# Loading the later queries of an attention–convolution kernel through SyncE in 1 KB f32 runs, and reordering their rows in the exponentials

## The chip, the cores and the metric

The kernel runs on one core of a Trainium2 chip. The time is device time in microseconds (us) from one launch, median of three runs. The profile is one execution of the same program taken by the hardware profiler. Engines are named as the profile names them: PE (TensorE, with PEld for its weight loads), DVE (VectorE), ACT (ScalarE), POOL (GpSimd), SP (SyncE, here only a queue that issues DMAs).

## The reference, cut to what matters

There are 8 batches, 12 heads, 448 rows and 64 elements per head. Attention is a softmax with an extra one in the denominator; its output, 448 x 768 per batch, goes into a gated layer with a circular convolution over the rows.

```
scores = q @ k.T / 8                      # per batch and head, 448 x 448
e      = exp(scores)
x      = (e / (sum(e) + 1)) @ v           # heads side by side: 448 x 768   (max shift cancels)
proj   = x @ w_proj                       # 768 x 2304
x1, x2, x3 = proj split in three
y      = x1 * x3 * irfft(rfft(x2) * rfft(filter))
out    = y @ w_out                        # 448 x 768, f32
```

## The kernel before, in words

**Units.** Heads are taken in pairs, six pairs to a batch, 48 pairs in all; pair i is pair i % 6 of batch i // 6. Per pair the scores stand transposed: keys on the partitions, the 448 queries along the free side. Keys 0 to 383 of each head are three tiles of 128 rows (t = 1, 2, 3, both heads at once); the last 64 keys of the two heads share a fourth tile (t = 0). `scores(t)` (L766 to L773) writes them to PSUM, `exps(t)` (L775 to L784) turns them to bf16 in SBUF with the scale folded in: 128 x 896 for t = 1, 2, 3 and 128 x 448 for t = 0. `out_rests` and `out_rest` (L792 to L810) multiply by v; the exponentials are the stationary operand there, 128 queries at a time, so **the order of the queries in an exponential tile is the order of the rows of x**. A column of ones beside v gives the sums, and `norm` (L812 to L824) divides, on DVE, into the tile `xb`.

**Getting x transposed.** The dense layer wants x with channels on the partitions (`xT`). For batches in `XALL`, and for the first five pairs of batches 2, 3 and 4, this is a DMA transpose issued by SP, three pairs (or two) at a time (`x_dma`, L886 to L893). For all other pairs PE transposes four blocks of 128 x 128 (`x_pe`, L898) and DVE or ACT copies them out of PSUM (`x_back`, L905 and L907): all of batches 0 and 1 and the last pair of batches 2, 3 and 4, so 15 pairs.

**Loading q, k and v.** Batches 0 and 1 (`staged`) come in f32 through SP into a ring of staging rooms, are cast on POOL (the first pair on DVE) and turned on PE. There a partition p of the q room holds the four queries 4p to 4p+3 of a head, one run of 1 KB; the copy out of PSUM (L488 to L493) puts the 448 columns back in row order. Batches 2 to 7 (`loaded`, L524 to L602) take k and v the same way through five rooms, cast on POOL, but are turned by DMA (`k_turn`). Their q is loaded by POOL-issued DMAs that cast on the way (`q_load`, L533): one strip of 112 consecutive rows for all twelve heads, in runs of 64 f32 elements, 256 bytes. A DMA transpose per strip (`q_turn`, L539) puts it in place already in row order. Four strips make a batch; batch 2 loads each in two halves, so there are 28 such loads and 28 such turns.

**Dense layer.** Per batch: folds of xT on DVE (L947 to L955), a projection P (L978), spectra Z (L1005) with products on DVE (L1019, L1025), the gates G (L1051, with L1063 and L1066), the inverse transform I (L1090) with its unfolding, and the output O (L1163, L1175).

**Order.** Nothing is scheduled by hand line by line. Every step is a task with an engine, a cost, a priority (`want`), needs, and buffers taken and given; `Plan.run` (L72) walks a model of the five engines and of two DMA queues and gives each engine the first ready task by priority among the next 160. The result is one fixed, in-order program per engine, with semaphore waits. The constants at the top of the kernel (L270 to L291) only move priorities: `ATT` and `SLOT` for each batch's attention, `DENSE`, `PACE` and `FOLD` for its dense layer, `LEAD` and `AHEAD` for loads. `LOAD` also is an earliest time in the model for the five weight loads and the filter load that POOL issues. `LANDING` and the argument `run` model how long a DMA takes to land and how the two queues share the transfers.

Of the kernel before, what the change touches and what calls it, by code (L numbers as in the profile page):

```python
# [23 lines left out]
NHP = H // 2  # L24
SCALE = 1.0 / float(np.sqrt(DH))
# [16 lines left out]
class Plan:  # L42
# [8 lines left out]

    WINDOW = 160
    LAT = {"PE": 0.2, "ACT": 0.22, "DVE": 0.2, "POOL": 0.15, "SP": 0.0}
    LANDING = 1.8
    OPEN = 8
    BEGIN = 0.75

# [11 lines left out]
    def add(self, eng, cost, want, emit, need=(), make=(), take=(), give=(), dma=0.0, run=256, n=1, after=0.0, begun=(), late=0.0):  # L69
        self.tasks.append((want, len(self.tasks), eng, cost, emit, need, make, take, give, dma, after, run, n, begun, late))  # L70
# [186 lines left out]
def kernel(  # L257
# [13 lines left out]
    MAGIC = 12582912.0  # L271
    NSTAGED = 2
    SPIN = 38
    EARLY1 = 3.56
    ATT = [0.74, 31.12, 90.92, 107.97, 154.61, 193.46, 231.91, 282.14]
    SLOT = [2.70, 6.66, 5.08, 5.83, 4.70, 0.35, 4.90, 4.50]
    DENSE = [45.16, 85.16, 124.09, 170.16, 216.54, 256.31, 315.08, 409.78]
    PACE = [2.27, 2.24, 1.74, 2.16, 1.15, 2.13, 0.54, 0.88]
    FOLD = [-0.15, 0.76, -31.49, -25.60, 10.65, 0.32, 9.43, 0.88]
    BPS = 1.26  # L280
    RE1 = 16.91
    WT = 2.03
    FT = 18.78
    HALVED = (2,)
    AHEAD = [0, 0, 46.94, 46.01, 34, 34, 34, 34]
    LEAD = [-8.41, 6.91, 5.34, 23.10]
    LOADS = ((1, 0), (1, 1), ("F", None), (0, None), (2, None), ("O", None))
    LOAD = [36.34, 20.13, 13.48, 39.00, 39.88, 46.37]
    STEP = 4.27
    XALL = (5, 6, 7)  # L290
    FOLD0 = (39.83, 49.48, 37.97)  # L291

    const = ctx.enter_context(tc.tile_pool(name="const", bufs=1))
    wts = ctx.enter_context(tc.tile_pool(name="wts", bufs=1))
# [25 lines left out]
    kT = [const.tile([128, NHP, 4, 128], BF16, name=f"kT{i}") for i in range(2)]  # L320
    qT = [const.tile([128, NHP, S], BF16, name=f"qT{i}") for i in range(2)]
    vn = [const.tile([128, NHP, 7, DH + 1], BF16, name=f"vn{i}") for i in range(2)]
    ks = const.tile([128, NHP, 128], BF16, name="ks")

    es = [const.tile([128, 2 * S + REM], BF16, name=f"e{i}") for i in range(6)]
    er = [const.tile([128, S + REM], BF16, name=f"er{i}") for i in range(2)]
# [2 lines left out]


    KNAT, ROOM = NHP * 4 * 128, 1280
    nat = const.tile([128, max(KNAT + NST * D, 8 * ROOM)], BF16, name="nat")
    kn = nat[:, 0:KNAT].rearrange("p (g t c) -> p g t c", g=NHP, t=4)
    qn = nat[0:SP, KNAT : KNAT + NST * D].rearrange("p (t c) -> p t c", t=NST)
    nf = nat.bitcast(F32)

    def stage(g, at, n):
        o = g % 4 * ROOM + at
# [15 lines left out]
    def bank(hy):  # L354
        i = plan.banks[hy][0]
        return psum[:, 512 * i : 512 * i + 512]
# [167 lines left out]
    def loaded(b):  # L524

        i0 = b * NHP
        want = tau(i0) - AHEAD[b]
        parts = 2 if b in HALVED else 1
        size = NHP // parts
# [13 lines left out]

        def k_turn(hp):
# [6 lines left out]
        n = 0  # L551
        for part in range(parts):
            gs = slice(size * part, size * part + size)
            for st in range(NST):
                room = [("c" + w, i0 - 2) for w in "kqv"] if b == NSTAGED else [("qturn", b - 1, st)]
                add("POOL", 0.8 if parts > 1 else 0.95, want + STEP * n, lambda st=st, gs=gs: q_load(st, gs), need=room,
                    make=[("qn", b, part, st)], dma=1.3 / parts)
                n += 1
                add("SP", 1.3, want + 6.0 + STEP * n, lambda st=st, gs=gs: q_turn(st, gs), need=[("qn", b, part, st), last],
                    make=[("qturn", b, st)] + [("qT", i0 + i) for i in range(gs.start, gs.stop)], dma=0.6 / parts, late=0.7)  # L560
# [11 lines left out]

        for hp in range(NHP):
            g = i0 + hp
            for n, (name, x) in enumerate((("k", k), ("v", v))):
                slot = 2 * (g - NHP * NSTAGED) + n
                at = (KNAT + NST * D) // 2 + 384 * (slot % 5)
                src = nf[:, at : at + 384]
                old = slot - 5
                room = [("c" + "kv"[old % 2], NHP * NSTAGED + old // 2)] if old >= 0 else [  # L580
                    ("c" + w, i) for w in "kqv" for i in range(NHP * NSTAGED - 2, NHP * NSTAGED)]
# [177 lines left out]
    def attention(i):  # L759
# [15 lines left out]
        def exps(t):  # L775
            if t:
                P["e"][t] = e = es[(3 * i + t - 1) % 6]
                nc.scalar.activation(  # L778
                    e[:, 0 : 2 * S].rearrange("p (u n) -> p u n", u=2), pair(("sc", ("S", i, t)))[:, :, 0:S], AF.Exp,
                    scale=SCALE,  # L780
                )
            else:
                P["e"][t] = e = er[i % 2]
                nc.scalar.activation(e[:, 0:S], bank(("hy", ("S", i, t)))[:, 0:S], AF.Exp, scale=SCALE)  # L784

        def out_banks():
            return pair(("op", i))[:, :, 0 : NST * (DH + 1)].rearrange("p u (n d) -> p u n d", n=NST)
# [442 lines left out]
    with (  # L1230
# [54 lines left out]
            need=[("c" + x, g) for x in "kqv" for g in range(NHP * NSTAGED - NHP, NHP * NSTAGED - 2)], make=["zero kn"])  # L1285
        for (part, ch), at in zip(LOADS, LOAD):
            if part == "F":
                add("POOL", 1.6, at, filter_load, need=["ft", "bps"], make=["filt"], take=[("yT", "F")], dma=4.1, run=2600, n=3, after=at)
            elif part == "O":
                add("POOL", 0.95, at, wout_load, make=["wout"], dma=6.9, run=2600, after=at)  # L1290
            elif ch is None:
                add("POOL", 0.95, at, lambda part=part: wproj_load(part, None), make=[("w", part, 0), ("w", part, 1)], dma=6.9,
                    run=2600, after=at)
            else:
                add("POOL", 0.7, at, lambda part=part, ch=ch: wproj_load(part, ch), make=[("w", part, ch)], dma=3.5, run=2600, after=at)
        more_tables()
        filter_spectrum()
        for i in range(n_batches * NHP):
# [34 lines left out]
```

## Time and profile before

| what | value |
|---|---|
| median of 3 runs | 387.96 us (386.69 to 388.25) |
| span of the profiled execution, first to last instruction | 384.6 us |
| outside the span, median less span | 3.4 us (2.1 to 3.7 over the runs) |
| PE busy | 367.6 us |
| ACT busy, DVE busy, POOL busy | 264.9, 258.4, 113.9 us |
| bytes moved by DMA | 59.12 MB in 136109 packets |
| packets under 512 bytes | 100925 |
| POOL-issued queue / SP-issued queue, packets | 37184 / 98640 |

The page gives a span for the profiled execution and no launch time of its own; the difference to the median is what lies around the span. A line of the groups reads: line of the kernel, engine, operation, output <- inputs, shape, count, busy us, mean ns of one, then the idle time of the engine before them with what ended it. "L898" is line 898 of the kernel shown above. A matmul's duration is longer than the distance to the next one, since matmuls are pipelined; the chain of waits counts only the distance.

### The profile page before, as it was taken

Reading aid. Unit: us, or ns where it says so; the run is one execution under the profiler, and the core shown is the slowest. Engines: PE = TensorE matmul, PEld = TensorE weight load, DVE = VectorE, ACT = ScalarE, POOL = GpSimd, SP = SyncE. Lnnn points to the kernel's source line nnn. Section 1 sums busy time; section 2 is a strip of 40 time slices with the busy share of each in tenths; the row PEclk is TensorE's granted clock in tenths of the full one; section 3 lists DMA queues with packets and bytes.
Section 4 is the critical chain, followed back from the end, with each engine's and each line's share of the span. In section 5 each row is a group of like instructions: output and inputs, shape, how many; then the busy total and the mean of one; then the engine's idle time right before and its main releaser. Section 6 shows DMA issues by size and latency. Waiting matters only on the chain.

```text
span 384.6 us, 9596 instructions
## 1 busy us (share of the span) xinstructions
PE 367.6 (96%) x3720; PEld 235.1 (61%) x3720; DVE 258.4 (67%) x676; ACT 264.9 (69%) x460; POOL 113.9 (30%) x232
## 2 busy tenths in 40 slices
PE   8786999999999999999998999999999999999995
PEld 7554775566765566655754576555665567557652
DVE  6576749955788548974399758584577845971870
ACT  6686769545887869787767768687678875543543
POOL 5783942422762644543364331100000000000000
PEclk9998999999999999999999999999999999999999
DMA  8999999999999999999999952932302033103004
GB/s 209 241 205 250 212 215 214 150 184 194 241 213 196 173 290 233 198 151 258 264 248 127 232 134 77 201 84 82 84 3 43 22 103 84 43 0 124 0 2 164
DMA packets 136109, 59.12 MB, mean 154 GB/s; under 512 B 100925, under 2 KB 132480, under 8 KB 136064
## 3 DMA queue, kind: packets, MB, share of 16 engines
q1 hardware_dynamic: 98640, 48.74, 57.9%
q0 software_dynamic: 37184, 9.54, 27.8%
q8 instruction: 29, 0.48, 0.5%
q10 hardware_dynamic: 240, 0.23, 0.2%
q14 instruction: 16, 0.13, 0.1%
HBM read 43.86 MB, written 11.01 MB: 143 GB/s over the span
## 4 chain that ended last, share of the span: by engine, by line
PE 78%; DVE 12%; DMA 4%; issue 1%; ACT 1%; POOL 1%; SPq 1%; DVEq 0%; POOLq 0%
PE psum L1051 22%; PE psum L978 16%; PE psum L1163 14%; PE psum L804 9%; PE psum L771 7%; DMA filt<-in_moe_filter_fft_dram 3%; PE psum L1005 2%; DVE t L1019 2%; PE psum L773 2%; PE psum L1090 2%; DMA nat<-in_q_dram 2%; DVE yh L1025 2%; DVE g L1066 1%; PE psum L796 1%; DVE cv L1119 1%
## 5 line engine op out<-in xcount | busy, mean ns | idle before, releaser
L778 ACT ACTIVATE e<-psum 128x896 bf16<-128x896 f32 x144 | 125.4, 921 | 21.6 <-PE psum L771 20.7
L1051 PE MATMUL psum<-xT,wproj_bf 128*128 128x448 bf16 x576 | 121.4, 352 | 0.3 <-DVE g L1066 0.3
L1051 PEld LDWEIGHTS <-wproj_bf 128*128 128x128 bf16 x576 | 54.0, 97 | 44.6 <-issue 2.0
L978 PE MATMUL psum<-wproj_bf,xf 128*113 128x384 bf16 x384 | 69.7, 327 | 0.0
L978 PEld LDWEIGHTS <-xf 128*113 128x113 bf16 x384 | 49.4, 132 | 13.7 <-issue 2.2
L1163 PE MATMUL psum<-wout_bf,yT 128*128 128x384 bf16 x288 | 51.9, 326 | 0.1
L1063 ACT CAST x<-psum 128x448 bf16<-128x448 f32 x48 | 25.6, 534 | 33.7 <-PE psum L1051 33.5
L804 PE MATMUL psum<-vn,e 128*128 128x65 bf16 x1152 | 45.3, 195 | 0.0
L600 POOL CAST vn<-nat 128x192 bf16<-128x192 f32 x72 | 28.8, 428 | 47.5 <-DMA nat<-in_v_dram 32.7
L1066 DVE TENSOR_TENSOR g<-x,psum 128x448 bf16<-128x448 bf16 x48 | 29.5, 615 | 19.5 <-PE psum L1051 19.0
L804 PEld LDWEIGHTS <-e 128*128 128x128 bf16 x1152 | 39.6, 98 | 2.8
L771 PE MATMUL psum<-qT,kT 64*128 64x448 bf16 x288 | 41.2, 358 | 0.0
L1175 ACT COPY osb<-psum 128x384 f32<-128x384 f32 x56 | 26.1, 483 | 20.5 <-PE psum L1163 20.1
L1163 PEld LDWEIGHTS <-yT 128*128 128x128 bf16 x288 | 27.4, 98 | 19.1 <-DVE yT L1134 0.8
L1019 DVE TENSOR_TENSOR t<-xs,hrs 113x768 bf16<-113x768 bf16 (+1 forms) x64 | 34.5, 577 | 1.6 <-ACT xs L1013 1.6
L817 DVE TENSOR_SCALAR rec<-psum 128x8 f32<-128x8 f32 x48 | 7.7, 161 | 40.5 <-PE psum L804 35.5
L819 DVE TENSOR_TENSOR xb<-psum,rec 128x512 bf16<-128x512 f32 x48 | 33.2, 691 | 1.7
L990 DVE CAST x<-psum 113x384 bf16<-113x384 f32 x32 | 17.7, 553 | 23.9 <-PE psum L978 23.7
L534 POOL DMA_DIRECT2D nat<-in_q_dram x28 | 24.8, 888 | 28.6 <-DMA wproj_bf<-in_moe_w_proj_dram 11.2
L1013 ACT CAST xs<-psum 113x384 bf16<-113x384 f32 (+1 forms) x64 | 28.0, 491 | 4.3 <-PE psum L1005 4.2
L992 ACT CAST x<-psum 113x384 bf16<-113x384 f32 x32 | 15.3, 480 | 21.8 <-PE psum L978 21.5
L784 ACT ACTIVATE er<-psum 128x448 bf16<-128x448 f32 x48 | 26.7, 556 | 2.9 <-PE psum L773 2.8
(109 smaller groups left out, 440.5 us busy)
## 6 DMA issues: line engine op xcount, KB each, us to landing
nat<-in_k_dram SPq DMA_DIRECT2D x48, 192.0 KB, 5.4
nat<-in_v_dram SPq DMA_DIRECT2D x48, 192.0 KB, 5.8
out_dram<-osb SPq DMA_DIRECT2D x24, 384.0 KB, 3.0
nat<-in_q_dram POOLq DMA_DIRECT2D x20, 168.0 KB, 6.9
nat<-in_q_dram SPq DMA_DIRECT2D x11, 224.0 KB, 7.3
wproj_bf<-in_moe_w_proj_dram POOLq DMA_DIRECT2D x2, 1152.0 KB, 17.5
rests<-in_k_dram SPq DMA_DIRECT2D x8, 192.0 KB, 6.4
rests<-in_v_dram SPq DMA_DIRECT2D x8, 192.0 KB, 7.1
```

What stands on the lines that cost most here:

```text
L600: nc.gpsimd.tensor_copy(vn[b % 2][:, hp, 4 * u : 4 * u + 3, 0:DH], sv[:, u])
L771: nc.tensor.matmul(sc[:, u, 0:S], kT[b % 2][c, hp, t, :], qT[b % 2][c, hp, :])
L778: nc.scalar.activation(e[:, 0 : 2 * S].rearrange("p (u n) -> p u n", u=2), pair(("sc", ("S", i, t)))[:, :, 0:S], AF.Exp, scale=SCALE,)
L784: nc.scalar.activation(e[:, 0:S], bank(("hy", ("S", i, t)))[:, 0:S], AF.Exp, scale=SCALE)
L804: nc.tensor.matmul(out_bank(u)[:, n, :], P["e"][1 + t][:, u * S + n * 128 : u * S + n * 128 + 128], vn[b % 2][:, hp, 4 * u + t, :], start= ...
L819: nc.vector.tensor_tensor(W["xb", b][:, hp].rearrange("p n (u d) -> p u n d", u=2), op[:, :, :, 0:DH], rec[:].unsqueeze(3).to_broadcast([1 ...
L978: nc.tensor.matmul(pps[:FQ, :DCH], W["xf", b][:, pg, kt, 0:FQ], wproj_bf[:, kt, D + ch * DCH : D + (ch + 1) * DCH], start=(kt == 0), stop= ...
L1013: nc.scalar.copy(L["xs", par, ch][:K, pg % 2, :], L["Z", pg, ch][:K, :DCH])
L1019: nc.vector.tensor_tensor(t[:K], L["xs", par, ch][:K], h, op=ALU.mult)
L1051: nc.tensor.matmul(p[:, :S], wproj_bf[:, kt, 2 * part * D + dt * 128 : 2 * part * D + (dt + 1) * 128], xT()[:, kt, 0:S], start=(kt == 0), ...
L1066: nc.vector.tensor_tensor(g[:, dt, :], L["x1", dt], p[:, :S], op=ALU.mult)
L1163: nc.tensor.matmul(ops[:n, :DCH], y[:, dt, 0:n], wout_bf[:, dt, ch * DCH : (ch + 1) * DCH], start=(dt == 0), stop=(dt == NDT - 1),)
```

## The change

1. **q of batches 2 to 7.** `q_load` by POOL with the cast in the DMA is gone. SP now loads, per head pair, f32 in 1 KB runs (four consecutive queries of a head per partition) into one of two rooms; POOL casts 112 x 512 into `qn`; SP issues a DMA transpose for one pair (batch 2) or three pairs (the others). The columns of `qT` then stand in the order j * 112 + n for query 4n + j.
2. **Row order.** For these batches the exponential reads PSUM in sequence and writes SBUF with a step of four elements (8 bytes), so that the exponential tile is again in row order. Scores, sums and products with v are otherwise as before.
3. **x.** `XALL` goes from (5, 6, 7) to (1, ..., 7): only batch 0's six pairs are still turned on PE.
4. **Rooms.** The natural-layout buffer grows; one of the five k/v rooms now lies in the tile `ks`, which batch 1's turns still read, so the first five k/v loads of batch 2 wait for all casts of pairs 9 to 11 and for the turns of pairs 6 to 11; q loads wait for the same casts.
5. **Order.** All priorities are new, `LANDING` is 2.2 and `run` of the weight loads 1500 (filter, w_proj and w_out). The gate weights (part 0) and half of part 1 may now start at about 18 to 20 us of the model, the filter at 27, w_out at 82.

```diff
-    LANDING = 1.8
+    LANDING = 2.2
...
-    EARLY1 = 3.56
-    ATT = [0.74, 31.12, 90.92, 107.97, 154.61, 193.46, 231.91, 282.14]
-    SLOT = [2.70, 6.66, 5.08, 5.83, 4.70, 0.35, 4.90, 4.50]
-    DENSE = [45.16, 85.16, 124.09, 170.16, 216.54, 256.31, 315.08, 409.78]
-    PACE = [2.27, 2.24, 1.74, 2.16, 1.15, 2.13, 0.54, 0.88]
-    FOLD = [-0.15, 0.76, -31.49, -25.60, 10.65, 0.32, 9.43, 0.88]
-    BPS = 1.26
-    RE1 = 16.91
-    WT = 2.03
-    FT = 18.78
-    HALVED = (2,)
-    AHEAD = [0, 0, 46.94, 46.01, 34, 34, 34, 34]
-    LEAD = [-8.41, 6.91, 5.34, 23.10]
+    EARLY1 = -5.85
+    ATT = [-63.37, 36.20, 83.38, 128.18, 122.21, 218.64, 210.09, 292.26]
+    SLOT = [1.36, 6.40, 8.21, 8.91, 11.38, 2.68, 4.29, 4.12]
+    DENSE = [50.42, 77.73, 144.20, 160.20, 213.12, 281.73, 315.75, 367.72]
+    PACE = [2.71, 3.56, 3.39, 2.66, 1.44, 0.79, 2.71, 1.39]
+    FOLD = [3.84, -32.37, -15.20, -28.40, -33.99, 9.69, -1.20, -1.70]
+    BPS = -25.34
+    RE1 = 46.00
+    WT = -31.32
+    FT = 0.83
+    LEAD = [4.72, 83.18, 8.95, -3.90, 7.63, -20.62, 94.14]
     LOADS = ((1, 0), (1, 1), ("F", None), (0, None), (2, None), ("O", None))
-    LOAD = [36.34, 20.13, 13.48, 39.00, 39.88, 46.37]
-    STEP = 4.27
-    XALL = (5, 6, 7)
-    FOLD0 = (39.83, 49.48, 37.97)
+    LOAD = [36.80, 17.95, 27.44, 19.56, 37.20, 81.70]
+    XALL = (1, 2, 3, 4, 5, 6, 7)
+    FOLD0 = [58.39, 87.97, 7.09]
...
-    ks = const.tile([128, NHP, 128], BF16, name="ks")
+    ks_flat = const.tile([128, NHP * 128], BF16, name="ks")
+    ks = ks_flat.rearrange("p (g c) -> p g c", g=NHP)
...
+    rooms = [nf[:, KNAT + 384 * i : KNAT + 384 * i + 384] for i in range(KV - 1)] + [ks_flat.bitcast(F32)[:, :]]
+    qrooms = [nf[:, KNAT + 384 * (KV - 1) + 512 * i :][0:SP, 0:512] for i in range(QS)]
...
-        def q_load(st, gs):
-            nc.gpsimd.dma_start(
-                qn[:, st, 128 * gs.start : 128 * gs.stop].rearrange("p (h d) -> p h d", d=DH),
-                q[b, 2 * gs.start : 2 * gs.stop, st * SP : (st + 1) * SP, :].rearrange("h p d -> p h d"),
-            )
-
-        def q_turn(st, gs):
+        staged_done = [("c" + w, i) for w in "kqv" for i in range(NHP * NSTAGED - 3, NHP * NSTAGED)]
+
+        def q_turn(hp):
             nc.sync.dma_start(
-                qT[b % 2][:, gs, st * SP : (st + 1) * SP], qn[:, st, 128 * gs.start : 128 * gs.stop], transpose=True
+                qT[b % 2][:, hp : hp + few].rearrange("p g (j n) -> p (g j) n", j=NST),
+                qn[:, hp : hp + few].rearrange("p g j c -> p (g j c)"),
+                transpose=True,
             )
...
+            add("SP", 0.52, tau(g) - LEAD[4],
+                lambda hp=hp, qsrc=qsrc: nc.sync.dma_start(
+                    qsrc.rearrange("p (u c) -> p u c", u=2),
+                    q[b, 2 * hp : 2 * hp + 2].rearrange("u (p j) d -> p u (j d)", j=NST),
+                ),
+                need=[("cq", g - QS)] if n >= QS else staged_done, make=[("sq", g)], dma=0.75, run=1024)
+            add("POOL", 0.65, tau(g) - LEAD[5],
+                lambda hp=hp, qsrc=qsrc: nc.gpsimd.tensor_copy(
+                    qn[:, hp].rearrange("p j (u d) -> p u j d", u=2),
+                    qsrc.rearrange("p (u j d) -> p u j d", u=2, j=NST),
+                ),
+                need=[("sq", g)] + ([("qT", g - NHP)] if b > NSTAGED else staged_done), make=[("cq", g)])
+            if hp % few == 0:
+                gs = range(g, g + few)
+                add("SP", 1.3, tau(g) - LEAD[6], lambda hp=hp: q_turn(hp), need=[("cq", i) for i in gs] + [last],
+                    make=[("qT", i) for i in gs], dma=0.5 * few, late=0.7)
...
-                nc.scalar.activation(
-                    e[:, 0 : 2 * S].rearrange("p (u n) -> p u n", u=2), pair(("sc", ("S", i, t)))[:, :, 0:S], AF.Exp,
-                    scale=SCALE,
-                )
+                to, of = e[:, 0 : 2 * S], pair(("sc", ("S", i, t)))[:, :, 0:S]
+                if b < NSTAGED:
+                    to = to.rearrange("p (u n) -> p u n", u=2)
+                else:
+                    to = to.rearrange("p (u n j) -> p u j n", u=2, j=NST)
+                    of = of.rearrange("p u (j n) -> p u j n", j=NST)
+                nc.scalar.activation(to, of, AF.Exp, scale=SCALE)
...
-                nc.scalar.activation(e[:, 0:S], bank(("hy", ("S", i, t)))[:, 0:S], AF.Exp, scale=SCALE)
+                to, of = e[:, 0:S], bank(("hy", ("S", i, t)))[:, 0:S]
+                if b >= NSTAGED:
+                    to, of = to.rearrange("p (n j) -> p j n", j=NST), of.rearrange("p (j n) -> p j n", j=NST)
+                nc.scalar.activation(to, of, AF.Exp, scale=SCALE)
```

More of the change, by code (lines that the diff above doesn't have):

```diff
@@ L331 @@
     KNAT, ROOM = NHP * 4 * 128, 1280
-    nat = const.tile([128, max(KNAT + NST * D, 8 * ROOM)], BF16, name="nat")
+    KV, QS = 5, 2
+    nat = const.tile([128, max(2 * KNAT + (KV - 1) * 768 + QS * 1024, 8 * ROOM)], BF16, name="nat")
     kn = nat[:, 0:KNAT].rearrange("p (g t c) -> p g t c", g=NHP, t=4)
-    qn = nat[0:SP, KNAT : KNAT + NST * D].rearrange("p (t c) -> p t c", t=NST)
+    qn = nat[0:SP, KNAT : 2 * KNAT].rearrange("p (g t c) -> p g t c", g=NHP, t=NST)
     nf = nat.bitcast(F32)
+    rooms = [nf[:, KNAT + 384 * i : KNAT + 384 * i + 384] for i in range(KV - 1)] + [ks_flat.bitcast(F32)[:, :]]
+    qrooms = [nf[:, KNAT + 384 * (KV - 1) + 512 * i :][0:SP, 0:512] for i in range(QS)]
     def stage(g, at, n):
@@ L526, in loaded @@
         i0 = b * NHP
-        want = tau(i0) - AHEAD[b]
-        parts = 2 if b in HALVED else 1
-        size = NHP // parts
         few = 1 if b == NSTAGED else 3
         last = ("S", i0 - NHP - 1, 3)
-        def q_load(st, gs):
-            nc.gpsimd.dma_start(
-                qn[:, st, 128 * gs.start : 128 * gs.stop].rearrange("p (h d) -> p h d", d=DH),
-                q[b, 2 * gs.start : 2 * gs.stop, st * SP : (st + 1) * SP, :].rearrange("h p d -> p h d"),
-            )
-        def q_turn(st, gs):
+        staged_done = [("c" + w, i) for w in "kqv" for i in range(NHP * NSTAGED - 3, NHP * NSTAGED)]
+        def q_turn(hp):
             nc.sync.dma_start(
-                qT[b % 2][:, gs, st * SP : (st + 1) * SP], qn[:, st, 128 * gs.start : 128 * gs.stop], transpose=True
+                qT[b % 2][:, hp : hp + few].rearrange("p g (j n) -> p (g j) n", j=NST),
+                qn[:, hp : hp + few].rearrange("p g j c -> p (g j c)"),
+                transpose=True,
             )
@@ L549, in k_turn @@
             )
[L551 to L560, printed above, removed]
         for n, (name, x) in enumerate((("k", k), ("v", v))):
@@ L574, in loaded @@
             g = i0 + hp
+            n = g - NHP * NSTAGED
+            qsrc = qrooms[n % QS]
+            add("SP", 0.52, tau(g) - LEAD[4],
[14 more added lines that the diff above has]
+                    make=[("qT", i) for i in gs], dma=0.5 * few, late=0.7)
             for n, (name, x) in enumerate((("k", k), ("v", v))):
                 slot = 2 * (g - NHP * NSTAGED) + n
[L577 to L581, printed above, removed]
+                src = rooms[slot % KV]
+                old = slot - KV
+                room = [("c" + "kv"[old % 2], NHP * NSTAGED + old // 2)] if old >= 0 else staged_done + [
+                    ("T", i) for i in range(NHP * NSTAGED - NHP, NHP * NSTAGED)]
                 add("SP", 0.52, tau(g) - LEAD[0] + 0.1 * n,
@@ L1287 @@
             if part == "F":
-                add("POOL", 1.6, at, filter_load, need=["ft", "bps"], make=["filt"], take=[("yT", "F")], dma=4.1, run=2600, n=3, after=at)
+                add("POOL", 1.6, at, filter_load, need=["ft", "bps"], make=["filt"], take=[("yT", "F")], dma=4.1, run=1500, n=3, after=at)
             elif part == "O":
-                add("POOL", 0.95, at, wout_load, make=["wout"], dma=6.9, run=2600, after=at)
+                add("POOL", 0.95, at, wout_load, make=["wout"], dma=6.9, run=1500, after=at)
             elif ch is None:
                 add("POOL", 0.95, at, lambda part=part: wproj_load(part, None), make=[("w", part, 0), ("w", part, 1)], dma=6.9,
-                    run=2600, after=at)
+                    run=1500, after=at)
             else:
-                add("POOL", 0.7, at, lambda part=part, ch=ch: wproj_load(part, ch), make=[("w", part, ch)], dma=3.5, run=2600, after=at)
+                add("POOL", 0.7, at, lambda part=part, ch=ch: wproj_load(part, ch), make=[("w", part, ch)], dma=3.5, run=1500, after=at)
         more_tables()
```

## The prediction

> **What bounds the kernel now.** I read the page's engine shares and slices first, then busy time by stage, then the chain that ended last with the waits inside it, and last the rows that the diff touches. Engines and slices:
>
> ```profile
> PE 367.6 (96%) x3720; PEld 235.1 (61%) x3720; DVE 258.4 (67%) x676; ACT 264.9 (69%) x460; POOL 113.9 (30%) x232
> PE   8786999999999999999998999999999999999995
> PEclk9998999999999999999999999999999999999999
> DMA  8999999999999999999999952932302033103004
> ```
>
> PE is full from the sixth slice to the last. The DMA engines are full too up to slice 22, but that need not cost anything, and the chain says that it mostly doesn't:
>
> ```profile
> PE 78%; DVE 12%; DMA 4%; issue 1%; ACT 1%; POOL 1%; SPq 1%; DVEq 0%; POOLq 0%
> ```
>
> The 4% of DMA are two pieces, both before 33 us: the second pair's staged q (6.41 us) and the filter (10.68 us). No transfer of batches 2 to 7 is on the chain. By stage (columns: stretch, its length, busy us of PE, PEld, DVE, ACT, POOL, granted clock, DMA share, GB/s):
>
> ```profile
> 0.00:40.00 40.00, 31.35 (x452) 23.42 (x453) 26.02 (x74) 27.07 (x39) 24.97 (x65) 0.96 1.05 226
> 40.00:96.00 56.00, 54.76 (x540) 35.39 (x540) 39.49 (x103) 38.04 (x68) 23.49 (x41) 1.00 1.45 194
> 96.00:192.00 96.00, 95.67 (x1034) 60.36 (x1030) 66.47 (x167) 76.06 (x129) 45.65 (x88) 1.00 1.30 222
> 192.00:320.00 128.00, 125.81 (x1300) 78.03 (x1299) 88.19 (x234) 95.29 (x163) 19.80 (x39) 1.00 0.57 111
> ```
>
> PE idles 8.65 us in the first 40, then 1.24, 0.33 and 2.19, and about 4.5 at the very end. So a gain must come out of PE's own work or the start; between 40 and 320 there are 3.8 us of PE idle to be had. Two waits are worth seeing, the one of the start and the one in front of PE's transposes of x:
>
> ```profile
> 32.99 0.96 DVE L716 TENSOR_TENSOR uw<-filt 113x1536 bf16<-113x1536 bf16 x1 [2.61 <-DMA filt<-in_moe_filter_fft_dram]
> 35.04 0.40 PE L898 MATMUL psum<-ident_bf,xb 128*128 128x128 bf16 x4 [2.93 <-DVE xb L819]
> 205.72 0.40 PE L898 MATMUL psum<-ident_bf,xb 128*128 128x128 bf16 x4 [1.36 <-DVE xb L819]
> ```
>
> DVE stood for the filter, the normalisation of a finished pair stood behind it, PE stood for that, and the clock fell to 0.79 in the next 8 us.
>
> **The change, part by part**, against the span of 384.6 us; the median lies 3.4 above it, and I carry that unchanged.
>
> *x by DMA.* Nine pairs (batch 1's six, one each of batches 2 to 4) lose four PE transposes each. The chain counts 0.22 us for such a group (40.42 to 40.64), so 9 x 0.22 = 2.0 us of the bounding engine go. PE's waits in front of them after 40 us are 2.6 us in all (0.82 at 67, 0.37 at 73, 1.36 at 205.7, 0.05). What is late next there is DVE, which is on the chain at 57 to 73 and 192 to 214 us, so I take half, 1.3; the ends are 0 and 2.6. Nine copies of 0.39 us leave DVE. In exchange SP issues two more transposes (batch 1) and three larger ones; twelve such cost 1.44 us of SP at the median and land 3.8 us later. Batch 1's last x is ready at 74 us and its first projection runs at 91.9, so 15 us cover that latency; for batch 4 there is no such cover in the trace, and up to 5 us of landing would come before its folds, unless its gates are late anyway.
>
> *q.* Off POOL: 28 issues of 0.89 us, 24.8 us, and its two stands behind weight loads (11.2 us). Onto POOL: 36 casts of 112 x 512, 0.615 us each in the staged batches, 22.1 us. So POOL is even, at 30% busy. Onto SP: 36 loads of 0.46 us, 16.7 us; the turns go from 28 at a median of 1.24 us, 35 us, to 6 of one pair and 10 of three, by the k turns' 1.2 and 2.13 us 28.5 us. With some 3 us for x, SP gains about 13 us on the 160 that its issues take between 40 and 250. Room is there, but SP is in order: behind a turn that waits for three casts stand the next loads, x turns and stores. Packets: 32256 of 256 bytes become 8064 of 1 KB, and x adds 36 blocks of 128 rows. The POOL queue's 27.8% of 16 engines' span over 37184 packets is 46 ns per packet, so some 93 us of full DMA go and perhaps 25 + 10 come. All of that lies beside PE, which idles 3.8 us in that stage: I count it at nothing. Its cover is the dense work of batches 0 and 1, on which PE lived from 72 to 85 us while no scores were issued; if the loads came later than that, PE would stand.
>
> *Longer wait for batch 2.* Its first k and v loads were issued at 45.3 to 52.4 us; now they need batch 1's last turn, on PE at 56.9. Landing (6 us), casts (1.8 us a pair) and turns (1.2 us and 4 to 6 to land) put its first scores near 72. Before, its casts began only at 68.1, since POOL stood behind weight loads, and its scores came at 85. Nothing.
>
> *POOL against DVE.* With POOL quiet after 258 us the spectrum product takes 0.55 us and its sum 0.35; from 45 to 258 they take 0.59 and 0.45. Over all DVE operations with two SBUF inputs this is 11 us for 59 us of POOL casts, 0.19 us per us. If issues cost DVE nothing, 22 us of new casts add 4 us to DVE, of which the two DVE stretches (37 of 213 us) hold 0.7. Of the copies that leave, three are pieces of the chain in those stretches: 0.39 + 0.30 + 0.30 = 1.0. Net a gain of 0.3. The Trainium skill (SBUF — State Buffer, the section on who interferes with whom) speaks against this part: a DVE instruction with two SBUF inputs and a GpSimd instruction that reads SBUF exclude each other, the later one blocks fully. By it every cast that met such an operation would cost up to its 0.6 us: 36 x 0.6 x 37/213 = 3.8 us on the stretches in place of 0.7 (estimate), and the sum would shrink by 3. The trace shows the effect at a fifth of that.
>
> *Exponentials.* 108 of 0.921 and 36 of 0.556 us, 119.5 us in all, now write with a step of 8 bytes. No row of before shows ACT writing with a step. The nearest: ACT's copy of q (L491), which reads PSUM with a step, 0.527 us, against its copy of x in sequence (L905), 0.535: nothing. Farther: the same copies on DVE, 0.618 against 0.387: 60% more. The engine is the same in the first, so I take nothing, and keep 60% as the other end. Less than nothing is excluded: as many elements pass as before. The Trainium skill (SBUF — State Buffer, the note on cachelines) says that accesses run at full rate while two of them fall in one line of 16 bytes, which for bf16 holds here; by it the term is zero too. No run so far shows it.
>
> *The start.* The filter load moves from 13 to 27 us of the model, so the spectrum should no longer stand in front of batch 0's normalisation. What that stall cost is 2.9 us of PE and the slow clock behind it: scores and products from 36.0 to 39.2 took 1.4 us more than the same groups elsewhere (1.44 against 0.86 for 24 products, 0.86 against 0.5 for the scores). That is 4.3 us at most. Against it, the gate weights (2.36 MB read) go ahead of the filter and of batch 1's loads: at 226 GB/s these are 10.4 us of transfers for whoever stands behind. The tables' DVE work (about 1 us) also moves ahead of the sines; PE's first 2.8 us of idle come from loads and hide it. Ends -4.3 and +10.4; I take -2, since the loads behind the weights belong to batch 1, which has batch 0's remaining pairs in front of it.
>
> *The end.* The last 20 us are a chain DVE, PE, store; no operation of it changes. Nothing, plus or minus 2 by order.
>
> Sum: -2.0 (work) - 1.3 (waits) - 0.3 (DVE) - 2 (start) = -5.6 us: span 379.0, time 382.4.
>
> **Rivals.**
> *Exponentials slow down (slower).* Between 96 and 192 us ACT is busy 76.1 of 96 us, 50.7 of them exponentials: at 1.39 times, 1.28 us each, ACT is full there and takes PE's place. At the DVE price of 1.6 times, 109 us of exponentials between 96 and 320 grow by 65.5 against 52.7 us of ACT idle: 13 us more, 382.4 + 13 = 395. For it: no row shows the write. Against: L491.
> *The start gets worse (slower).* Batch 1's loads stand behind the gate weights, PE has no scores and no projection between 30 and 50 us: 8 us lost in place of 2 won, 392.4. For it: POOL's stands of 4.3 and 6.9 us behind weight loads, and staged loads that land in 7.3 us when DMA is full. It decides from 6 us of additional PE idle before 60 us. SP's new loads blocking each other would look the same later.
> *All was hidden (same).* Only PE's 2.0 us go and the order gives a little back: 386 to 388.
> *The start gets much better.* The idle and the filler matmuls of the first 40 us (8.65 and 6.9 us) shrink by half as well: 372.
>
> **How the numbers follow.** Forecast (376 to 386): 0.52. Better start: 0.08. Same: 0.10. Slow exponentials: 0.10. Start or queue worse: 0.20. A measurement here tells about 0.5% (2 us) from no change. Faster 0.60, same 0.10, slower 0.30. Leaving out one in ten at either side, the range runs from 373 to 396; the forecast's own is 376 to 386.
>
> **What would show it.** L778 stays within 3% of 921 ns; L898 counts 24; PE idle after 40 us falls under 3 us to the last slice; L716 no longer waits 2.6 us for the filter, and the clock stays at 1.0 before 40 us; POOL's group for q is 36 casts at 0.62 us. Wrong if L778 passes 1.2 us, if PE idles over 15 us before 60 us, or if xT's folds wait for DMA in batches 2 to 4.

## The result, and the profile after

The changed kernel takes 484.83 us (484.45 to 487.52) against 387.32 for the kernel before on the same chip: a ratio of 1.253 [1.246, 1.260], 97.5 us slower, where 382.4 was forecast and 396 was the range's upper end. The profiled execution's span is 482.7 us, 98.1 more than before.

First the page's engine shares and slices of the changed kernel:

```profile
PE 391.6 (81%) x3700; PEld 242.0 (50%) x3700; DVE 254.0 (53%) x667; ACT 405.3 (84%) x460; POOL 107.4 (22%) x240
PE   8987996798596777677787987687779887789996
ACT  6784889969969999999979699998999989964453
PEclk9998999899989999999999899899899998999999
DMA  8999968994976995993965403282110113010013
```

PE did 20 instructions fewer, and its row of nines, which began with the sixth slice and went nearly to the end, is gone; most slices of ACT's row, from the seventh to the 35th, are nines now. ACT has as many instructions as before (460) and is busy 140.4 us longer (405.3 against 264.9). The groups of before and then, of the changed kernel, the chain that ended last and the groups name the instruction:

```profile
L778 ACT ACTIVATE e<-psum 128x896 bf16<-128x896 f32 x144 | 125.4, 921 | 21.6 <-PE psum L771 20.7
L784 ACT ACTIVATE er<-psum 128x448 bf16<-128x448 f32 x48 | 26.7, 556 | 2.9 <-PE psum L773 2.8
```

```profile
ACT 41%; PE 36%; issue 8%; DMA 7%; DVE 4%; POOL 2%; SPq 1%; ACTq 0%; POOLq 0%; DVEq 0%
L785 ACT ACTIVATE e<-psum 128x896 bf16<-128x896 f32 x144 | 260.6, 1921 | 15.0 <-PE psum L772 15.0
L791 ACT ACTIVATE er<-psum 128x448 bf16<-128x448 f32 x48 | 52.6, 1096 | 2.6 <-PE psum L774 2.5
```

ACT had 1% of the chain and has 41%. The exponentials (L778 and L784 before, L785 and L791 now) took 921 and 556 ns; these means of 1921 and 1096 mix two kinds. One answer for the line L785 (minimum, median and maximum in ns, first and last start) separates them:

```profile
L785 ACT ACTIVATE e<-psum x144: 912/2216/2377, 8.5 to 424.7; 128x896 bf16<-128x896 f32 x144
```

With batches 0 and 1 (36 of the 144) still at 0.92, the 108 stepped ones average (144 x 1921 - 36 x 921) / 108 = 2254 ns, 2.45 times as long; the 36 smaller ones by the same working 1276, 2.3 times. By stage (columns: stretch, its length, busy us of PE, PEld, DVE, ACT, POOL, granted clock, DMA share, GB/s):

```profile
0.00:40.00 40.00, 32.34 (x484) 24.27 (x485) 23.29 (x74) 28.90 (x42) 24.05 (x65) 1.00 1.05 237
40.00:96.00 56.00, 48.68 (x501) 30.87 (x497) 38.45 (x97) 46.70 (x62) 19.48 (x38) 0.94 0.95 189
96.00:192.00 96.00, 74.88 (x679) 45.13 (x678) 46.27 (x115) 85.82 (x90) 31.60 (x67) 0.98 0.80 185
192.00:320.00 128.00, 98.77 (x920) 59.25 (x919) 64.82 (x165) 117.78 (x117) 32.24 (x71) 0.97 0.61 145
320.00:420.00 100.00, 79.80 (x713) 46.56 (x713) 42.24 (x116) 95.34 (x93) 0.00 (x0) 0.97 0.18 49
```

ACT is busy 89, 92 and 95% of the last three stages. PE, which idled 0.33 us between 96 and 192 before, idles 21.1 there, and its waits say for whom (us in total, times, longest):

```profile
PE psum L772 <- ACT e L785: 22.0, 29, 1.6
PE psum L803 <- ACT e L785: 8.3, 6, 1.7
PE psum L1058 <- ACT e L785: 7.7, 6, 2.0
PE psum L1012 <- ACT e L785: 7.5, 8, 1.8
```

Scores (L772) wait until an exponential has freed their PSUM. The first products with v (L803), the gates (L1058) and the spectra (L1012) stand until an exponential is done too. Two things are as the change meant them: 24 transposes of x are left on PE (L905) of 60, and the q casts on POOL (L568) are 36 at 643 ns.

### The profile page after: what moved, and what is told of

Its sections match the earlier page's. It is cut to its first block, busy times and chain, and to the rows that moved or that the text cites. A ratio compares the mean times of both kernels' runs of the same rounds, so it can differ in the third digit from the quotient of the medians.

```text
span 482.7 us, 9536 instructions
## 1 busy us (share of the span) xinstructions
PE 391.6 (81%) x3700; PEld 242.0 (50%) x3700; DVE 254.0 (53%) x667; ACT 405.3 (84%) x460; POOL 107.4 (22%) x240
## 4 chain that ended last, share of the span: by engine, by line
ACT 41%; PE 36%; issue 8%; DMA 7%; DVE 4%; POOL 2%; SPq 1%; ACTq 0%; POOLq 0%; DVEq 0%
ACT e L785 29%; PE psum L1058 15%; PE psum L985 7%; PE psum L1170 6%; ACT er L791 4%; DMA nat<-in_k_dram 4%; PE psum L811 3%; ACT osb L1182 3%; PE psum L772 2%; DMA nat<-in_q_dram 1%; ACT x L1070 1%; ACT cr L1106 1%; PE psum L1097 1%; ACT xs L1020 1%; PE psum L1012 1%
## 5 line engine op out<-in xcount | busy, mean ns | idle before, releaser
L785 ACT ACTIVATE e<-psum 128x896 bf16<-128x896 f32 x144 | 260.6, 1921 | 15.0 <-PE psum L772 15.0
L1058 PE MATMUL psum<-xT,wproj_bf 128*128 128x448 bf16 x576 | 128.1, 363 | 11.6 <-ACT e L785 7.7
L1058 PEld LDWEIGHTS <-wproj_bf 128*128 128x128 bf16 x576 | 55.3, 100 | 61.6 <-issue 22.3
L772 PE MATMUL psum<-qT,kT 64*128 64x448 bf16 x288 | 44.5, 358 | 23.9 <-ACT e L785 22.0
L1170 PE MATMUL psum<-wout_bf,yT 128*128 128x384 bf16 x288 | 54.7, 328 | 10.7 <-ACT e L785 6.6
L791 ACT ACTIVATE er<-psum 128x448 bf16<-128x448 f32 x48 | 52.6, 1096 | 2.6 <-PE psum L774 2.5
L1070 ACT CAST x<-psum 128x448 bf16<-128x448 f32 x48 | 27.6, 574 | 16.5 <-PE psum L1058 16.4
L1182 ACT COPY osb<-psum 128x384 f32<-128x384 f32 x56 | 28.5, 530 | 14.5 <-PE psum L1170 14.0
L772 PEld LDWEIGHTS <-kT 64*128 64x128 bf16 x288 | 12.1, 94 | 49.2 <-issue 47.6
L568 POOL CAST nat<-nat 112x512 bf16<-112x512 f32 x36 | 22.9, 643 | 56.0 <-DMA nat<-in_q_dram 55.9
L601 POOL CAST vn<-nat 128x192 bf16<-128x192 f32 x58 | 21.4, 390 | 45.2 <-PE psum L811 42.2
```

The source lines that it names most:

```text
L772: nc.tensor.matmul(sc[:, u, 0:S], kT[b % 2][c, hp, t, :], qT[b % 2][c, hp, :])
L785: nc.scalar.activation(to, of, AF.Exp, scale=SCALE)
L791: nc.scalar.activation(to, of, AF.Exp, scale=SCALE)
L1058: nc.tensor.matmul(p[:, :S], wproj_bf[:, kt, 2 * part * D + dt * 128 : 2 * part * D + (dt + 1) * 128], xT()[:, kt, 0:S], start=(kt == 0), ...
L1070: nc.scalar.copy(L["x1", dt], p[:, :S])
L1170: nc.tensor.matmul(ops[:n, :DCH], y[:, dt, 0:n], wout_bf[:, dt, ch * DCH : (ch + 1) * DCH], start=(dt == 0), stop=(dt == NDT - 1),)
```

## The experiments

The theory after the result: the stepped write of the exponentials is the whole loss, and the rest of the change is worth the forecast's -5.6 us. The rivals: the new loads come late and the time goes there, whatever ACT does; or the reordering costs ACT on either side. All ratios are to the kernel before on the same chip, with a 95% interval.

**The stepped write alone**, put into the kernel before (the rows of the output of batches 2 to 7 come out permuted):

```diff
+                if b < NSTAGED:
+                    to = to.rearrange("p (u n) -> p u n", u=2)
+                else:
+                    to = to.rearrange("p (u n j) -> p u j n", u=2, j=NST)
+                    of = of.rearrange("p u (j n) -> p u j n", j=NST)
+                nc.scalar.activation(to, of, AF.Exp, scale=SCALE)
...
+                if b >= NSTAGED:
+                    to, of = to.rearrange("p (n j) -> p j n", j=NST), of.rearrange("p (j n) -> p j n", j=NST)
```

> The kernel before, in its own order and with its own loads, with only the exponentials of batches 2 to 7 written with a step of 4 elements (their rows, and so the output's rows of these batches, come out permuted). Write theory: 2.2 and 1.27 us, ACT busy 265 + 108 x 1.3 + 36 x 0.71 = 431 us, time 470 to 500 us, as long as the changed kernel or longer. Order theory: exponentials slow as well, but below 430 us, since this order leaves ACT 120 us idle.

479.56 us, 1.246 [1.240, 1.253]. Its engines, and its stage from 96 to 192 us:

```profile
PE 388.1 (81%) x3720; PEld 239.2 (50%) x3720; DVE 259.1 (54%) x676; ACT 404.5 (85%) x460; POOL 112.0 (24%) x232
96.00:192.00 96.00, 74.78 (x721) 44.45 (x719) 48.99 (x125) 94.43 (x92) 33.33 (x66) 0.98 0.84 150
```

The loads are those of before, and ACT is busy 94.43 of 96 us. These few lines cost 94.8 us by themselves; late loads are out as the main cause. The changed kernel's remainder is some 3 us, with the wrong sign; the intervals of the two ratios overlap, so these 3 us are not clear of noise.

**The same reordering on the read side.** The changed kernel, in which the exponential reads PSUM with a step of 112 elements (448 bytes) and writes in sequence. What is computed stays the same.

```diff
-                    to = to.rearrange("p (u n j) -> p u j n", u=2, j=NST)
-                    of = of.rearrange("p u (j n) -> p u j n", j=NST)
+                    to = to.rearrange("p (u n j) -> p u n j", u=2, j=NST)
+                    of = of.rearrange("p u (j n) -> p u n j", j=NST)
...
-                    to, of = to.rearrange("p (n j) -> p j n", j=NST), of.rearrange("p (j n) -> p j n", j=NST)
+                    to, of = to.rearrange("p (n j) -> p n j", j=NST), of.rearrange("p (j n) -> p n j", j=NST)
```

> The changed kernel with the row order made on the other side of the exponential: it reads PSUM with a step of 112 f32 elements and writes SBUF in sequence; all else, the order too, is the changed kernel's. Write theory (a stepped bf16 write by ACT is what costs): exponentials back at 0.92 and 0.56 us, ACT busy about 265 us, PE over 93% busy, and the rest of the change shows by itself, 376 to 392 us. Pattern theory (any access pattern out of sequence costs, on either side): exponentials stay over 1.8 us, 480 us. Order theory (the new order and the loads cost most of the 98 us, slow exponentials only fill the gaps): exponentials 0.92 us but 430 us or more.

389.07 us, 1.011 [1.007, 1.016]; run again later, 387.97 us, 1.006 [1.002, 1.009]:

> The read-side kernel once more, on the same chip as the two others, to compare them with: 1.007 to 1.016 of before.

The exponentials of the first of these runs:

```profile
L785 ACT ACTIVATE e<-psum 128x896 bf16<-128x896 f32 x144 | 126.3, 925 | 22.5 <-PE psum L772 22.4
L791 ACT ACTIVATE er<-psum 128x448 bf16<-128x448 f32 x48 | 26.7, 556 | 5.4 <-PE psum L774 5.4
```

They are back at 925 and 556 ns: reading PSUM with that step costs ACT nothing, so "either side" falls too. But all that is left of the change makes the kernel 0.6 to 1.1% slower, not 1.4% faster. That remainder is taken up below.

**Which steps cost.** The kernel before, its exponentials of batches 2 to 7 written with another pattern for each head pair of a batch (results permuted; the time as a whole means nothing):

```diff
...
+                elif hp == 0:
+                    nc.scalar.activation(*stepped(2), AF.Exp, scale=SCALE)
+                elif hp == 1:
+                    nc.scalar.activation(*stepped(4), AF.Exp, scale=SCALE)
+                elif hp == 2:
+                    nc.scalar.activation(*stepped(8), AF.Exp, scale=SCALE)
...
+                elif hp == 0:
+                    nc.scalar.activation(*runs(4, 2), AF.Exp, scale=SCALE)
...
```

> The kernel before, in its own order; the exponentials of batches 2 to 7 take another pattern for each of the six head pairs, so the rows of their exponentials, and the output, are permuted for all but the sequential ones. 128 x 896: steps of 2, 4, 8, 16 and 32 elements on the write side, and a step on the read side with the write in sequence. 128 x 448: write in runs of 2, 4, 8 and 16 elements, each run 4 runs from the last, a step on the read side, and a step of 4 on the write side. Cost by separate write (each element out of sequence is its own write): 2.2 us for all five steps, 1.27 us for single elements, and runs of 2 and more fall in proportion to 0.6 us. Cost by 16-byte line: 0.92 us at steps of 2 and, were it not measured otherwise, 4, and more only from 8. Cost by distance: growing from step 2 to step 32. Read side: 0.92 and 0.56 us by the write theory, over 1.8 and 1.1 by the pattern theory.

Its groups, in this order: in sequence, a step of 2, 4, 8, 16 and 32 bf16 elements, in sequence with the read stepped; then of the small size in sequence, in runs of 2 elements that lie 16 bytes apart, and with a step of 4:

```profile
L782 ACT ACTIVATE e<-psum 128x896 bf16<-128x896 f32 x36 | 31.7, 924 | 6.3 <-PE psum L771 6.1
L784 ACT ACTIVATE e<-psum 128x896 bf16<-128x896 f32 x18 | 20.4, 1186 | 0.5 <-PE psum L771 0.4
L786 ACT ACTIVATE e<-psum 128x896 bf16<-128x896 f32 x18 | 38.3, 2223 | 1.7 <-PE psum L771 1.7
L788 ACT ACTIVATE e<-psum 128x896 bf16<-128x896 f32 x18 | 74.0, 4330 | 0.6 <-PE psum L771 0.6
L790 ACT ACTIVATE e<-psum 128x896 bf16<-128x896 f32 x18 | 71.7, 4156 | 0.0
L796 ACT ACTIVATE e<-psum 128x896 bf16<-128x896 f32 x18 | 72.5, 4212 | 0.0
L792 ACT ACTIVATE e<-psum 128x896 bf16<-128x896 f32 x18 | 16.3, 963 | 3.9 <-PE psum L771 3.9
L803 ACT ACTIVATE er<-psum 128x448 bf16<-128x448 f32 x12 | 6.7, 557 | 1.3 <-PE psum L773 1.3
L805 ACT ACTIVATE er<-psum 128x448 bf16<-128x448 f32 x6 | 3.5, 579 | 2.3 <-PE psum L773 2.3
L816 ACT ACTIVATE er<-psum 128x448 bf16<-128x448 f32 x6 | 7.1, 1182 | 1.8 <-PE psum L773 1.8
```

The two sequential sizes give 0.19 us fixed and 0.82 ns per element. Above the fixed part a step of 2, 4 and 8 costs 1.1, 2.3 and 4.6 ns per element: about double with each doubling up to 16 bytes, and no more beyond. Pairs of elements (4 bytes) that lie 16 bytes apart cost nothing to speak of (579 against 557); runs of 4 and 8 elements took 591 and 631. Of the rules set out beforehand the cost per separate write has the right size for a step of 4 (2.2 us), but none has this doubling.

**How much slower ACT may become.** The kernel before with a step of 2 (rows permuted):

```diff
+                    to = to.rearrange("p (u n j) -> p u j n", u=2, j=2)
+                    of = of.rearrange("p u (j n) -> p u j n", j=2)
...
+                    to, of = to.rearrange("p (n j) -> p j n", j=2), of.rearrange("p (j n) -> p j n", j=2)
```

> The kernel before with the exponentials of batches 2 to 7 written with a step of 2 elements in place of 4 (rows permuted as there): a smaller dose of the same cost. From the table 1.18 us for 128 x 896, so 108 x 0.26 = 28 us for these, and some 36 x 0.13 = 5 us for 128 x 448: ACT busy about 300 us. If the prediction read the point rightly at which ACT takes over (1.39 times in the tightest stretch, and this is 1.28), ACT stays under 95% busy between 96 and 192 us and the time rises by no more than 6 us, to 385 to 393. If every us on ACT shows in the time, as from step 4 on (140 us more on ACT, 95 us more time), it rises by some 22 us, to 407 or more.

386.57 us, 1.007 [1.003, 1.012]. The large exponentials, and the stage from 96 to 192:

```profile
L784 ACT ACTIVATE e<-psum 128x896 bf16<-128x896 f32 x144 | 152.0, 1122 | 16.5 <-PE psum L771 15.7 <-DVE xf L961 0.3
96.00:192.00 96.00, 94.32 (x994) 58.74 (x992) 66.30 (x165) 84.66 (x128) 44.64 (x85) 1.00 1.33 214
```

The stepped exponentials take (144 x 1122 - 36 x 921) / 108 = 1189 ns, 1.29 times as long; ACT is busy 23 us longer in all and 88% of this stage, and PE loses only 1.35 us of it. At this dose, with ACT not yet full, most of these 23 us are hidden. No run lies between 1.29 and some 2.4 times, so the point at which the loss sets in is not measured.

**x by DMA alone.** The kernel before, nothing else than

```diff
-    XALL = (5, 6, 7)
+    XALL = (1, 2, 3, 4, 5, 6, 7)
```

> The kernel before with XALL = (1, ..., 7) alone: batches 1 to 4 get all of x by DMA transpose. By the prediction's terms 2.0 us of PE work, 1.3 of waits and some DVE go: 383 to 385 us. Rival (the landing of the transposes stands before the folds of batches 1 to 4): 388 to 396 us.

398.12 us, 1.036 [1.030, 1.042]: more than even the rival had said. The longest of PE's waits, and its stage from 40 to 96:

```profile
PE psum L1051 <- DMA xT<-xb: 9.1, 3, 6.9
40.00:96.00 56.00, 48.62 (x531) 30.39 (x530) 32.66 (x86) 37.04 (x64) 18.57 (x33) 0.98 1.36 184
```

With the old priorities the gates of the first batches wait for the DMA that took the place of PE's transposes. In the read-side version, with the new priorities, PE has no such wait among its longest. So this part alone loses with the old priorities. What it is worth by itself with new ones was not tried.

**q alone.** The read-side version with `XALL = (5, 6, 7)` as before, and priorities set anew for it:

```diff
-    XALL = (1, 2, 3, 4, 5, 6, 7)
+    XALL = (5, 6, 7)
```

> The q part alone: the read-side kernel with x transposed as in the kernel before (XALL = (5, 6, 7)) and priorities set anew for that. The prediction had the q part at nothing, so 0.995 to 1.005 of before. If the q part is what costs (POOL casts against DVE, more loads on SP), about 1.01, as with all parts; then x by DMA is worth nothing or little. If x by DMA costs, this is below the read-side kernel.

390.10 us, 1.012 [1.007, 1.017], beside 1.006 [1.002, 1.009] for the read-side version on the same chip. So the loss stays without x by DMA: it lies in the part with q, the rooms and the order that go with it. The read-side version is 0.6% faster than q alone, which by the two intervals is anything from nothing to 1.3%; that is what x by DMA may be worth, as far as two different orders can say.

**What of the q path costs?** Four runs, none of which settles it. First, in the same order, POOL casts 8 of the 512 columns and fills the rest with a constant, so POOL hardly reads q (the scores of batches 2 to 7 are not the reference's):

```diff
-                lambda hp=hp, qsrc=qsrc: nc.gpsimd.tensor_copy(
+                lambda hp=hp, qsrc=qsrc: (
+                    nc.gpsimd.tensor_copy(qn[:, hp, 0, 0:8], qsrc[:, 0:8]),
+                    nc.gpsimd.memset(qn[:, hp].rearrange("p j c -> p (j c)")[:, 8:512], 0.1),
...
```

> The read-side kernel, same order, where POOL casts only the first 8 of 512 columns of each q tile of batches 2 to 7 and fills the rest with a constant (so the scores of these batches are not those of the reference): POOL still waits for the load and still writes the tile, but hardly reads SBUF. Theory (POOL's casts stop DVE, and a train of them cost the 2.1 us at 160 us): no sum of products (the line that writes yh) over 1.5 us, DVE's two-input operations at 45 to 258 us lose 11 to 13 us to POOL in place of 17, and 1 to 4 us of the 4 that this kernel lies above the one before go. Rival (late loads and turns alone set it): DVE relieved, time within 1 us of the read-side kernel's, 1.1% above before.

386.21 us, 1.001 [0.997, 1.006], on another chip than the read-side version, so by the ratios 0.4 to 1.0% better, but the interval overlaps with both of the read-side version's and with before. DVE's operations with two SBUF inputs stood 16.0 us above their quiet durations (those after 258 us) between 45 and 258 us in the read-side version, and 13.4 in its repeat; they stand 9.8 above them here, near the kernel before (11.0). So DVE is relieved; what that brings in time is at the edge of what can be told.

If it were POOL against DVE, the cast could go to ACT, which has room (priorities set anew):

```diff
...
-            add("POOL", 0.65, tau(g) - LEAD[5],
-                lambda hp=hp, qsrc=qsrc: nc.gpsimd.tensor_copy(
+            add("ACT", 0.5, tau(g) - LEAD[5],
+                lambda hp=hp, qsrc=qsrc: nc.scalar.copy(
...
```

> The read-side kernel with the q casts of batches 2 to 7 on ACT instead of POOL, priorities set anew for that (the order differs). ACT gains 36 copies of about 0.6 us, some 20 us of the 120 it has idle; POOL loses 24 us of casts that read SBUF, and DVE's two-input operations should lose about 11 us to POOL as in the run without the q read. Contention theory: PE idle between 96 and 192 us falls under 2 us and the time is 0.5 to 1.5% below the read-side kernel's, level with before or under it. Rival (late loads and the order set it): as the read-side kernel or worse, since ACT now stands in order behind the q loads.

390.58 us, 1.013 [1.007, 1.019]. DVE was relieved here too (7.1 us above the quiet durations) and the time is no better: ACT, in order, stood 21.6 us for q loads in front of its casts. This version has another order of work, so it doesn't show what DVE's share is either.

Last, whether SP's queue is what is short: the read-side version without the output stores of batches 0 to 3, and the kernel before without the same ones as the control:

```diff
+            if b < 4:
+                return
```

> The read-side kernel without the output stores of batches 0 to 3 (their output is not written); every other instruction in its place. SP is in order: a q turn whose casts were done at 110.8 us was issued at 114.6, behind a k turn, four loads and a store, and landed at 121.2, when PE had stood 1.6 us. Queue theory (SP's in-order queue makes the q turns late): some 12 to 14 us of issues leave SP between 60 and 250 us, q turns come earlier, PE idles under 2 us between 96 and 192 us, the time falls by 2 to 4 us, to before's or under it. Rival (loads from memory and DVE set it): within 0.4% of the read-side kernel.

> The control: the kernel before without the same stores. If stores on SP cost in general, it gains as much as the other, 2 to 4 us; if only the q loads make SP too full, it stays within 0.4% of before.

385.72 us, 1.005 [1.000, 1.009], and 383.19 us, 0.995 [0.991, 0.998]. Against 1.006 to 1.011 with its stores the one gains 0.1 to 0.7%. The control gains 0.5% by its ratio, 0.1% by another choice among the runs of before, which are scattered there from 379.88 to 390.00 us. Set beside each other, on the same chip, the two differ by 0.7% (385.72 against 383.19), as the read-side version and before do with their stores (0.6 to 1.1%): nothing shows that the new q path needs room on SP more than the kernel before does.

## Why the prediction was wrong, by its steps

**The step that failed is "Exponentials. ... I take nothing."** The term put at nothing measured 1.33 us for each of the 108 large exponentials (2254 ns less 921) and 0.72 for each of the 36 small ones, and ACT was busy 140.4 us longer. Neither of the two rows behind the term shows a write with a step. L491 on ACT and L493 on DVE are the same copy of q: it reads PSUM with a step and writes SBUF in sequence, where the change does the reverse. The rows of before, each with the copy of x in sequence below it:

```profile
L491 ACT COPY qT<-psum 128x448 bf16<-128x448 bf16 x1 | 0.5, 527 | 0.0
L905 ACT COPY xT<-psum 128x448 bf16<-128x448 bf16 x2 | 1.1, 535 | 2.3 <-PE psum L898 2.3
L493 DVE COPY qT<-psum 128x448 bf16<-128x448 bf16 x11 | 6.8, 618 | 5.3 <-PE psum L472 5.2
L907 DVE COPY xT<-psum 128x448 bf16<-128x448 bf16 x13 | 5.0, 387 | 5.5 <-PE psum L898 5.5
```

The read-side run measures L491's kind of access in the exponentials at 925 ns and the table the change's at 2223. DVE's row, held for the outer end, had the right sign by luck, since it shows a stepped read that ACT gets for nothing; its 1.6 was too low by far against 2.45. The Trainium skill (SBUF — State Buffer, the note on cachelines) was quoted with two hits per 16-byte line being enough for full rate; with a step of 4 there are two, and the write took 2.4 times as long, and with a step of 2 there are four, and it took 1.28 times as long. The measurement decides: the note's rule does not hold for these writes.

**The rival was right in mechanism and place, and its price was mis-sized.** It said: ACT fills the stage from 96 us on and takes PE's place from 1.39 times on. At 1.29 times the cost was 0.7%, at 2.45 ACT was the engine that bounds, 89 to 95% busy. Its own sum, with the measured factor of about 2.4 for both sizes together, gives 109 x 1.4 - 52.7 = 100 us, close to the measured 98; with 1.6 it gave 13. Part of that closeness is luck: ACT's busy time grew by 140.4 us, not 153, and 42.3 us of its idle time were used up (119.7 before, 77.4 now), not 52.7; the two misses cancel. The input that was far off is the factor. "L778 passes 1.2 us" was named as what would show it.

**PE's work, -2.0:** L905 of the changed kernel (PE's transposes of x, L898 before) counts 24, so 9 x 0.22 us did leave PE. The gain doesn't show in the whole: PE idles 17.0 us before (384.6 less 367.6), 20.7 in the read-side version's first run (387.6 less 366.9) and 16.4 in its repeat (385.0 less 368.6).

**PE's waits, -1.3:** those in front of the transposes of x shrank from 6.4 us over the whole span (L898) to 1.8 (L905 of the read-side version), but others took their place (below). The folds wait for DMA, as the forecast named for a sign that it is wrong: DVE stands 6.3 us for xT in the read-side version, 3.7 of it at 111 us and 2.1 at 134, against 2.3 before (8.7 in the repeat); PE had other work in these places.

**The start, -2:** half right. The filter's stand is gone: L717 waited for no DMA, and the read-side version kept a clock of 1.00 before 40 us in its first run (0.96 in its second). But a staged q load of batch 1 now stands behind the gate weights, issued just before it, as the rival of the start had it. Two stretches of the read-side version's first run and the second of them in the repeat (columns as above), and then pieces of the first run's chain that ended last (start, us, what):

```profile
40.00:48.00 8.00, 6.27 (x95) 4.81 (x94) 5.65 (x19) 3.69 (x5) 2.91 (x7) 1.00 1.19 259
96.00:192.00 96.00, 91.39 (x937) 56.15 (x935) 67.43 (x159) 69.81 (x119) 46.69 (x98) 0.98 1.13 254
96.00:192.00 96.00, 92.51 (x943) 57.16 (x942) 64.51 (x162) 70.30 (x121) 46.89 (x98) 0.98 1.12 253
```

```profile
25.53 18.87 DMA nat<-in_q_dram
...
70.77 1.32 SPq L540
...
74.58 5.14 DMA nat<-in_q_dram
...
84.87 1.26 SPq L540
...
89.72 7.47 DMA nat<-in_k_dram
...
98.96 3.00 DMA nat<-in_q_dram
102.56 5.40 DMA nat<-in_k_dram
...
114.64 6.47 DMA qT<-nat
```

The first piece is that load: it stands 18.87 us on the chain where the filter stood 10.68, and PE then idles 1.7 us between 40 and 48. Up to 96 us PE idles 10.5 us in this run against 9.9 before: what the start won it lost again. In the repeat it idles 7.1, so there the start did gain, if less than it seems, since 97 filler matmuls stand in both runs where before had 81.

**q at nothing: wrong, by up to about 4 us.** "No transfer of batches 2 to 7 is on the chain" held for before. In the read-side version the chain goes through them from 63 to 121 us: k turns (SPq L540), q loads, k loads, POOL casts and a q turn, one behind the other in the order of SP and POOL, until PE waits 1.6 us at 121 us for qT. The repeat has the same pieces up to a q turn that lands at 119 us. PE fills most of that time with dense work, which is why it costs little, but from 96 to 192 it idles 4.6 us (3.5 in the repeat) where it idled 0.3. That this is the main part of the loss is likely, not shown: with q alone PE idles 2.5 us there with no q transfer on the chain, and in the repeat PE idles no more over the whole span than before. The forecast had named such blocking ("SP's new loads blocking each other would look the same later") without a price.

**Longer wait for batch 2, nothing:** this held. In the read-side version its loads were issued from 56.8 us on and its first scores ran at 74.0, against 84.8 before.

**POOL against DVE, -0.3:** the rate held on average, 16.0 us for some 88 us of casts, 0.18 per us (0.15 in the repeat), against 0.19. The average hid the one that hurts. The timeline of the read-side version, POOL and then DVE and PE (start, us, and the idle time before in brackets):

```profile
159.97 0.82 POOL L568 CAST nat<-nat 112x512 bf16<-112x512 f32 x1 [2.86 <-DMA nat<-in_q_dram]
160.74 0.50 POOL L589 CAST nat<-nat 128x384 bf16<-128x384 f32 x1
161.19 0.63 POOL L601 CAST vn<-ks 128x192 bf16<-128x192 f32 x2
161.77 0.50 POOL L554 CAST vn<-rests 128x384 bf16<-128x384 f32 x1
```

```profile
160.23 2.52 DVE L1032 TENSOR_TENSOR yh<-t 112x384 bf16<-112x384 bf16 x2
```

```profile
163.34 0.58 PE L1097 MATMUL psum<-bt,yh 113*128 113x113 bf16 x8 [2.11 <-DVE g L1073]
```

Four casts in a row, the first released by a q load and the others queued behind it, lie beside a sum of 0.35 us that took 2.25 (2.52 for the two of this line); PE stood 2.11 us, and the clock was 0.79 from 160 to 168 us. In the kernel before the longest such sum was 0.78. The rule weighed in the prediction (SBUF — State Buffer, who interferes with whom: the later one blocks fully) fits this case, the fifth the average. In the repeat the longest was 0.95, so this place is chance.

**What stays open:** how the 2 to 4 us of the read-side version divide among late q turns, DVE behind POOL, the new order and the clock after a stand. Taking POOL's reads away gave a time that can't be told from that of before, but moving them to ACT did not, and q alone was as slow with no q transfer of the later batches on its chain. More q rooms, which would decouple the loads, weren't tried. No version that computes the whole result beat the kernel before.

## What to carry to other kernels

Put a reordering on the side of an ACT instruction that reads PSUM, not on the side that writes bf16 to SBUF with a step; a stepped read says nothing about a stepped write, even on the same engine. Before taking a row for the nearest one, check which of its two sides has the step. When a change lengthens an instruction that runs 108 times on an engine at 69%, work out at which factor that engine is full; if no row shows the new access, let the range reach well past that factor, or measure the one instruction first. An engine with slack takes a lengthening for almost nothing while it isn't full (1.29 times cost 0.7% here), and for most of it once it is (2.45 times: 140 us more on ACT, 98 us more time).

## What the runs showed of the hardware

- ACT writing single bf16 elements to SBUF: 1186, 2223, 4330, 4156 and 4212 ns for 128 x 896 with steps of 4, 8, 16, 32 and 64 bytes, against 924 in sequence. By an estimate from these numbers it is as if each 16-byte line written cost 4.5 ns, shared by the elements that follow each other into it; but pairs of 4 bytes, one to a line, would then take some 1.2 us for 448 elements and took 0.58. What decides between single elements and pairs was not tried.
- ACT reading PSUM with a step of 448 bytes: nothing (925 against 921, 556 against 556; 963 against 924 in the run with the table, among the long writes). DVE's copy of q, which reads PSUM with a step, took 618 ns against 387 for a copy of the same size in sequence, where ACT's took 527 against 535.
- In the run with the table, small exponentials just behind a write of 4.2 us were recorded with 0.89 us (the read-side form, 556 ns in the read-side run). Their records begin 0.5 to 0.6 us before the record of the write ahead of them ends (one at 109.02 us, the write ahead of it up to 109.62), so the longer record is overlap and not a cost of its own.
- A staged load of batch 1, issued some 4 to 5 us after the gate weights, stands 18.9 us on the read-side version's chain and 14.7 on the changed kernel's, where the two staged loads ahead of it stand 5.8 and 7.3 us. That the weights are the reason is inferred from their place; the filter's load, issued 1.4 us after that of 18.9 us, is as near.
